# A routed attention and FFN kernel: one more head pair in cluster order, with smaller conversion buffers

## The chip, the core and the metric

The kernel runs on one core of a Trainium2 chip. A core has five engines with a queue each: PE (matmul; its weight loads are listed apart as PEld), DVE (vector), ACT (scalar), POOL (GpSimd) and SP, which here only issues DMAs. Each queue is worked off in its own order, and engines meet at semaphores. The metric is the device time of one execution in microseconds, the median of three runs.

## The reference

Two blocks follow each other. Attention with routing (4 batches, 8 heads, 768 tokens, 64 values per head): each query and key is assigned to the nearest of 16 centroids of its head, and a query sees only keys of its own cluster.

```python
q_assign = np.argmax(np.einsum('bhsd,hcd->bhsc', q_n, c_n), axis=-1)
k_assign = np.argmax(np.einsum('bhsd,hcd->bhsc', k_n, c_n), axis=-1)
mask = q_assign[:, :, :, None] == k_assign[:, :, None, :]
scores = np.where(mask, scale * np.matmul(q, k.transpose(0, 1, 3, 2)), -1e9)
attn = softmax(scores)                      # over the keys
out = np.matmul(attn, v)
```

Then an FFN on the 3072 rows of 512 values: `h = x @ w_in` (512 by 2048), `g = max(h, 0) + alpha * min(h, 0)`, `g @ w_out` (2048 by 512). The weights arrive as 64-bit floats, and the kernel makes 32-bit ones of them on the chip.

## The kernel before, in words

**Pairs and steps.** Two heads are worked on together: pairs 0 to 15, four to a batch. The program is a list of *steps* (`steps`), three to a pair and a half of its queries (384), and the loops over `u` at the end write out the order of everything by hand: each step has five slots, `load_at` and `prep_at` say which load and which preparation falls in which, and `later(k, piece)` puts a piece k slots ahead. Nothing is reordered afterwards: each engine's queue holds its instructions as the loops wrote them. Batch 0 is steps 0 to 23 (first loop: four pairs with their first halves, *block 0*, then the second halves, *block 1*), batch 1 steps 24 to 47, batch 2 steps 48 to 62, batch 3 steps 63 to 74.

**Two ways to do a pair.** In general a pair is done in halves: scores of 6 key chunks (128 keys) against 384 queries for both heads (`score`, L784), exponentials on ACT (L805), a mask on DVE (L825; in batch 0 two extra matmuls L793 put the mask into the scores), row sums on DVE (`add_up`, `turn`, `rows_sums`), products with v (`weigh`, L939), and `normalise` (L1042) into the tiles `xT` that the FFN reads. The accumulator `vps` has one buffer: PE can't start the next pair's products before `normalise` has read it. Pairs 9 to 15 (`n >= NO`) are done *in cluster order*: queries and keys are sorted by cluster, and each key chunk is only compared with a window of 224 to 384 queries (`window`, `weigh_near` L972). That takes three steps for both halves. It costs an ordering ahead of time: `order_features` (two transposes L567), `order_sims` (four matmuls L575), `order_counts` (argmax, a scan L589), `order_begins` (two matmuls L601), `order_ranks`, `order_rows`, `order_clusters` on DVE (L609 to L645), and then 24 indirect DMAs from POOL (`order_scatter`, L675), which write rows of q, k and v to a scratch in DRAM by rank. They take the rows from two stage tiles that SP loads (L661, three DMAs a tile). `pace()` (a one-element copy on ACT, L651, and one on POOL, L652) keeps POOL from running ahead. `order_load` brings the sorted rows back (L688, L697, L706). At the end six transposes on PE (L1002), twelve indirect DMAs (L1011) and four loads (L1023) put the result in the old order again. `order_constants` makes, once, what the ordering needs: on POOL two iotas (L508, L511) and three pairs of an iota (L521) and a product (L523), on DVE a reduction (L531), five small instructions (L538 to L548) and three `shifts`. `ORDERS` holds the step in which each ordering begins, `LEADS` how many steps ahead the sorted rows are loaded.

**The conversion of the weights.** 32 pieces of 128x512 (`convert`), numbered 0 to 31, in batch 0: SP loads a piece (L247, 512 KB) into one of five raw tiles; *split* (L253, L255, DVE) takes the exponent into a buffer `power` and the mantissa into the weight tile; *scale* (L259, L261, ACT); *join* (L265, L268, DVE), after which the raw tile is free; *multiply* (L271, POOL), after which `power` is free. Scale comes four slots after split, join two after scale. `fetch` issues a load when a raw tile is free in program order. The list `converting` gives the pieces begun in each step of block 0; from step 12 on two begin in each step. w_in and w_out alternate by fours.

**The FFN.** `feeds` says after which step the FFN of a half of a batch may begin, and its 28 pieces are spread over the steps of the next block: `hidden` (four matmuls L1066, a copy on ACT L1072, a slope on DVE L1058) and `final` (four matmuls L1084, evacuated at L1090 or L1092). The first FFN piece stands in step 12, right after the products of pair 3. Batch 3's FFN comes last, in another form with fewer products (L1246, L1302).

**Memory.** `first_part` holds what only batch 0 needs (members, raw tiles, `cvt` with the exponent buffers); when it closes after step 23, `second_part` takes its room for five more exponential tiles, one `xT` tile (`xmore`) and all that the ordering uses.

The line that decides whether a step finds its piece:

```python
later(4 if len(stages) == 2 else 2, lambda: stages and advance(stages))
```

## Time and profile before

| | |
|---|---|
| median of three runs | 932.17 us (932.1 to 932.6) |
| the profiled execution | 932.13 us, its span 930.4 us |
| PE busy | 916.0 us, 98% |
| DVE busy | 654.3 us, 70% |
| ACT busy | 262.2 us, 28% |
| POOL busy | 389.1 us, 42% |
| granted TensorE clock | 1.00 in all stretches |
| batch 0: block 0 ends, block 1 ends | about 77 us, about 201 us |

A row of a group, a line or the timeline gives the line of the kernel, the engine, the operation, what is written from what, and how often; "busy" is the time in which the engine worked, and in square brackets stands how long the engine was idle ahead of the row and who released it. Lines named L784 and so on are those of the kernel before.

### The profile page before, as it was taken

How to read it: one execution, taken by the hardware profiler on the slowest of the kernel's cores; microseconds unless marked ns; L12 is line 12 of the kernel's file. 1: busy time of each engine (PE TensorE's matmuls, PEld its weight loads, DVE VectorE, ACT ScalarE, POOL GpSimd, SP SyncE). 2: the span in 40 equal slices, each digit the busy share in tenths (PEclk: the TensorE clock that was granted, in tenths of full speed). 3: DMA queues.
4: the chain of work that ended last, by engine and by line, in shares of the span. 5: the costliest groups of instructions: out<-in, count | busy, mean ns of one | idle time of the engine just before them, and what ended most of it. 6: DMA issues, size and time to landing. Idle time of an engine off the chain costs nothing.

```text
span 930.4 us, 11983 instructions
## 1 busy us (share of the span) xinstructions
PE 916.0 (98%) x3963; PEld 494.6 (53%) x3963; DVE 654.3 (70%) x1246; ACT 262.2 (28%) x660; POOL 389.1 (42%) x579
## 2 busy tenths in 40 slices
PE   8999999999999999999999999999999999999997
PEld 5534444445445454455555554555555555556886
DVE  5797788889769699598997899764647135598200
ACT  5764454223123122232222332122222121221000
POOL 2433232200006768587766787677723470000000
PEclk9999999999999999999999999999999999999999
DMA  8433659028001625453762283643511012000000
GB/s 301 132 123 93 148 128 159 18 56 179 26 1 51 153 73 145 88 107 85 156 133 42 50 136 96 142 87 95 97 37 27 12 38 54 1 0 1 23 23 26
DMA packets 226708, 77.71 MB, mean 84 GB/s; under 512 B 210752, under 2 KB 214544, under 8 KB 226640
## 3 DMA queue, kind: packets, MB, share of 16 engines
q1 hardware_dynamic: 217728, 62.72, 30.6%
q0 software_dynamic: 8064, 13.78, 4.7%
q8 instruction: 33, 0.54, 0.3%
q10 hardware_dynamic: 848, 0.39, 0.2%
q14 instruction: 35, 0.29, 0.1%
HBM read 52.25 MB, written 24.25 MB: 82 GB/s over the span
## 4 chain that ended last, share of the span: by engine, by line
PE 94%; DVE 4%; issue 1%; POOL 0%; ACT 0%; DVEq 0%; ACTq 0%; POOLq 0%
PE fps L1066 27%; PE fps L1084 27%; PE sps L784 7%; PE vps L939 7%; PE sps L1302 4%; PE sps L1246 4%; PE fps L784 3%; PE vps L1246 2%; PE vps L1302 2%; PE vps L972 1%; PE mps L972 1%; PE fps L1302 1%; PE fps L1246 1%; PE sps L793 1%; PE mps L894 1%
## 5 line engine op out<-in xcount | busy, mean ns | idle before, releaser
L1066 PE MATMUL fps<-xT,w_in_sb 128*128 128x384 f32 x768 | 259.3, 491 | 0.0
L1084 PE MATMUL fps<-w_out_sb,gT 128*128 128x512 f32 x576 | 254.1, 595 | 0.3 <-DVE gT L1058 0.3
L675 POOL DMA_INDIRECT scratch<-stage,off x168 | 181.3, 1079 | 67.1 <-DMA stage<-in_v_dram 29.5
L1066 PEld LDWEIGHTS fps<-xT,w_in_sb 128*128 128x128 f32 x768 | 142.3, 190 | 103.2 <-issue 4.9
L1084 PEld LDWEIGHTS fps<-w_out_sb,gT 128*128 128x128 f32 x576 | 107.5, 190 | 132.2 <-issue 122.6
L1072 ACT COPY gT<-fps 128x384 f32<-128x384 f32 x96 | 46.0, 479 | 235.9 <-PE fps L1066 235.9
L652 POOL COPY paced<-pace 1x1 f32<-1x1 f32 x204 | 55.0, 270 | 135.7 <-ACT pace L651 135.2
L1058 DVE SCALAR_TENSOR_TENSOR gT<-gT,alpha 128x384 f32<-128x384 f32 x96 | 61.5, 648 | 60.8 <-ACT gT L1072 60.7
L1011 POOL DMA_INDIRECT back<-rows,off x84 | 85.6, 1018 | 22.2 <-issue 16.5
L784 PE MATMUL sps<-qkT 64*128 64x384 f32 (+1 forms) x464 | 85.0, 485 | 0.0
L805 ACT ACTIVATE E<-sps 128x768 f32<-128x768 f32 (+1 forms) x76 | 56.3, 786 | 62.1 <-PE sps L793 39.7
L784 PEld LDWEIGHTS sps<-qkT 64*128 64x128 f32 x464 | 41.2, 186 | 38.6 <-issue 15.5
L825 DVE SCALAR_TENSOR_TENSOR more<-aq,key,more 128x384 f32<-128x384 bf16 (+2 forms) x116 | 60.4, 579 | 0.0
L939 PE MATMUL vps<-E,vt 128*64 128x384 f32 x292 | 54.2, 495 | 1.5 <-DVE xT L1042 1.5
L271 POOL TENSOR_TENSOR w_in_sb<-w_in_sb,power 128x512 f32<-128x512 f32 x16 | 26.9, 1684 | 67.4 <-DVE w_in_sb L268 67.4
L271 POOL TENSOR_TENSOR w_out_sb<-w_out_sb,power 128x512 f32<-128x512 f32 x16 | 22.5, 1411 | 56.0 <-DVE w_out_sb L268 56.0
L825 DVE SCALAR_TENSOR_TENSOR E<-aq,key,E 128x384 f32<-128x384 bf16 (+2 forms) x88 | 45.0, 569 | 0.6 <-ACT E L802 0.6
L835 DVE TENSOR_TENSOR acc<-acc,E 128x768 f32<-128x768 f32 x35 | 33.3, 951 | 14.5 <-ACT E L805 13.6
L907 DVE RECIPROCAL inverses<-mps 64x12 f32<-64x12 f32 (+1 forms) x42 | 10.5, 249 | 45.7 <-PE mps L894 39.8
L1090 ACT COPY y<-fps 128x512 f32<-128x512 f32 x18 | 10.6, 587 | 99.2 <-PE fps L1084 99.2
L1092 DVE TENSOR_TENSOR y<-y,fps 128x512 f32<-128x512 f32 x24 | 16.4, 682 | 27.6 <-PE fps L1084 27.6
L805 ACT ACTIVATE more<-sps 128x768 f32<-128x768 f32 (+1 forms) x40 | 29.2, 764 | 12.2 <-PE sps L784 11.8
(284 smaller groups left out, 1174.1 us busy)
## 6 DMA issues: line engine op xcount, KB each, us to landing
raw<-in_moe_w_in_dram SPq DMA_DIRECT2D x16, 512.0 KB, 5.2
raw<-in_moe_w_out_dram SPq DMA_DIRECT2D x16, 512.0 KB, 4.3
out_dram<-y SPq DMA_DIRECT2D x21, 256.0 KB, 2.4
qk<-scratch SPq DMA_DIRECT2D x56, 96.0 KB, 3.5
qk<-in_q_dram SPq DMA_DIRECT2D x48, 96.0 KB, 3.6
qk<-in_k_dram SPq DMA_DIRECT2D x48, 96.0 KB, 3.6
w_in_kept<-w_in_sb SPq DMA_DIRECT2D x8, 512.0 KB, 3.3
vt<-in_v_dram SPq DMA_DIRECT2D x9, 384.0 KB, 6.5
```

What stands on the lines that cost most here:

```text
L652: nc.gpsimd.tensor_copy(out=sorts["paced"], in_=token)
L675: nc.gpsimd.indirect_dma_start(out=scratch[n][1][h * NX + xx], out_offset=bass.IndirectOffsetOnAxis(ap=ranks[n][:, xx, h:h + 1], axis=0), ...
L784: nc.tensor.matmul(out=bank(ps, h, m), lhsT=qkT[r:r + D, S + c * P:S + (c + 1) * P], rhs=qkT[r:r + D, tokens], start=True, stop=not early_ ...
L805: nc.scalar.activation(out=E[:, :, 0:m], in_=ps[:, :, 0:m], func=AF.Exp, scale=SCALE)
L825: nc.vector.scalar_tensor_tensor(out=e, in0=of, scalar=keys[n][:, NJ + c, h:h + 1], in1=e, op0=ALU.is_equal, op1=ALU.mult)
L939: nc.tensor.matmul(out=po[r:r + D, 0:HS], lhsT=vts[n][:, h, c, :], rhs=e[:, h, :], start=(c == 0), stop=(c == NJ - 1))
L1011: nc.gpsimd.indirect_dma_start(out=to[i], out_offset=bass.IndirectOffsetOnAxis(ap=place[:, h, j:j + 1], axis=0), in_=rows[j // HJ][:, j % ...
L1058: nc.vector.scalar_tensor_tensor(out=gs[f], in0=gs[f], scalar=alpha[:, f:f + 1], in1=gs[f], op0=ALU.mult, op1=ALU.max)
L1066: nc.tensor.matmul(out=ps[:, 0:HS], lhsT=w_in_sb[:, c, f * P:(f + 1) * P], rhs=xTs[b, half][:, c, :], start=(c == 0), stop=(c == NCH - 1))
L1084: nc.tensor.matmul(out=ps[:, 0:DM], lhsT=gs[f][:, i * P:(i + 1) * P], rhs=w_out_sb[:, f, :], start=on and f == f0, stop=off and f == f0 + ...
L1246: nc.tensor.matmul(out=bank[to], lhsT=w_in_form(m, x, cc), rhs=rhs[:, cc, :], start=start and cc == 0, stop=cc == KH - 1, skip_group_check ...
L1302: nc.tensor.matmul(out=bank[to], lhsT=g_form(m, x, t), rhs=w_out_form(n, x), start=start and x == 0, stop=x == NQ - 1, skip_group_check=no ...
```

## The change

- Pair 7, the last of batch 1, is done in cluster order too, ahead of pairs 4 to 6: `ORDERED` is 7 and 9 to 15. Batch 1 takes 21 steps and the program 72; the second half of batch 1 has 9 steps.
- Its ordering begins in step 11, `order_constants` is called in step 10 (before: step 25), and the first loop takes pieces from `sorting` too: in steps 16 to 20 five scatters a step. Tiles for the ordering are there from the start (`ordc`, `ordp`, `order`, `pace`), so the conversion gets three raw tiles in place of five, and `cvt` two exponent buffers in place of three. For the first 12 conversions every third takes its exponent buffer from the room of the output rows (`ypool`).
- Once more than 12 conversions have begun, scale comes three slots after split and join one after scale. `converting` in steps 3 to 6 is 1, 1, 1, 2 (before: 2, 0, 2, 1; the sum is the same).
- The later orderings begin in steps 26, 29, 32, 35, 38, 53 and 57. Which `xT` tile lies in which pool changes, a separate pool `ordx` holds the second half's factors, and some slots move by one.

```diff
-    NO = WHOLE * NCH - 3
+    ORDERED = [2 * NCH - 1] + list(range(WHOLE * NCH - 3, B * NCH))
+    NO = ORDERED[1]
...
-    cvt = first_part.enter_context(tc.tile_pool(name="cvt", bufs=3))
+    cvt = first_part.enter_context(tc.tile_pool(name="cvt", bufs=2))
...
-    raw_tiles = [raws.tile([P, CW, 2], U32, name=f"raw{i}") for i in range(5)]
+    started = [0]
+    raw_tiles = [raws.tile([P, CW, 2], U32, name=f"raw{i}") for i in range(3)]
...
-            power.append(cvt.tile([P, CW], U32, name="power"))
+            i = started[0]
+            started[0] += 1
+            power.append(ypool.tile([P, DM], FP32, name="y").bitcast(U32)
+                         if i < NCH * 3 and i % 3 == 2 else
+                         cvt.tile([P, CW], U32, name="power"))
...
-            later(4 if len(stages) == 2 else 2, lambda: stages and advance(stages))
+            later((4 if len(stages) == 2 else 2) - (started[0] > NCH * 3),
+                  lambda: stages and advance(stages))
...
-        whole = [n for n in range(b * NCH, (b + 1) * NCH) if n >= NO]
-        rest = [n for n in range(b * NCH, (b + 1) * NCH) if n < NO]
+        whole = [n for n in range(b * NCH, (b + 1) * NCH) if n in ORDERED]
+        rest = [n for n in range(b * NCH, (b + 1) * NCH) if n not in ORDERED]
...
-            pool = sorts["xmore"] if (b, half) == (WHOLE - 1, 1) else xpool
+            pool = sorts["xmore"] if (b, half) in ((1, 1), (B - 1, 0)) else xpool
...
-    ORDERS = [26, 29, 35, 38, 41, 56, 60]
-    LEADS = [4, 3, 4, 4, 3, 3, 3]
+    ORDERS = [11, 26, 29, 32, 35, 38, 53, 57]
+    LEADS = [3, 4, 3, 4, 4, 3, 3, 3]
...
+        if u == ORDERS[0] - 1:
+            order_constants()
...
-        converting = 0 if u < 0 else (2, 0, 2, 2, 0, 2, 1, 1, 1, 1, 1, 1)[u] if u < UB else 2
+        converting = 0 if u < 0 else (2, 0, 2, 1, 1, 1, 2, 1, 1, 1, 1, 1)[u] if u < UB else 2
...
+            if sorting:
+                pace()
+            room = 1 + (i < 2)
+            while sorting and room:
+                scatters, piece = sorting.popleft()
+                piece()
+                room -= scatters
...
-        if u == TOGETHER + 1:
-            order_constants()
```

More of the change, by code (lines that the diff above doesn't have):

```diff
@@ L76 @@
     fast.enter_context(tc.manual_schedule())
+    sorts = {name: fast.enter_context(tc.tile_pool(name=name, bufs=bufs)) for name, bufs in
+             (("ordc", 1), ("ordp", 1), ("order", B * NCH - 2 * NCH), ("pace", 8))}
     first_part = fast.enter_context(ExitStack())
@@ L490 @@
     STAGES = 2
-    us, ranks, orders, scratch, sorts = {}, {}, {}, {}, {}
+    us, ranks, orders, scratch = {}, {}, {}, {}
     sorting = deque()
@@ L496, in second_part @@
         first_part.close()
-        for name, bufs in (("emore", 1), ("ordc", 1), ("ordp", 1), ("order", NP - NO),
-                           ("xmore", 1), ("byrow", 1), ("pace", 8)):
-            sorts[name] = fast.enter_context(tc.tile_pool(name=name, bufs=bufs))
+        for name in ("emore", "ordx", "xmore", "byrow"):
+            sorts[name] = fast.enter_context(tc.tile_pool(name=name, bufs=1))
         for i in range(5):
@@ L560, in order_constants @@
             later(5 + i, piece)
-        begins = ordc.tile([P, NP - NO], FP32, name="begins")
+        begins = ordc.tile([P, len(ORDERED)], FP32, name="begins")
         sorts.update(stage=stage, number=number, place=place, before=before, within=within,
@@ L609, in order_ranks @@
         nc.vector.tensor_tensor(out=begin, in0=ps[:, 0:2], in1=sorts["shift"], op=ALU.add)
-        nc.vector.tensor_copy(out=sorts["begins"][:, n - NO:n - NO + 1], in_=ps[:, 0:1])
+        i = ORDERED.index(n)
+        nc.vector.tensor_copy(out=sorts["begins"][:, i:i + 1], in_=ps[:, 0:1])
         nc.vector.scalar_tensor_tensor(out=count, in0=count, scalar=begin[:, 1:2],
@@ L734 @@
         for half in range(2) if rest else ():
-            if half and not whole:
+            if half and b < WHOLE - 1:
                 begun_at.append(len(steps))
             steps += [(n, half, s) for n in rest for s in range(SB)]
-            feeds[len(steps)] = [(b, 0), (b, 1)] if whole else [(b, half)]
+            feeds[len(steps)] = [(b, half)] if b < WHOLE - 1 else [(b, 0), (b, 1)]
     begun_at.append(len(steps))
@@ L877, in rows_sums @@
     def rows_sums(n, half):
-        near = n >= NO
+        near = n in ORDERED
         if not near or half == 0:
@@ L911, in spread_out @@
     def spread_out(n, half, inv):
-        pool = sorts["ordp"] if n >= NO and half else rdp
+        pool = sorts["ordx"] if n in ORDERED and half else rdp
         rd = rds[n, half] = pool.tile([P, HS], FP32, name="rd")
@@ L1340, in room_for_y @@
         def room_for_y():
-            t = sorts["xmore"].tile([P, NCH, HS], FP32, name="xT").rearrange(
+            t = xpool.tile([P, NCH, HS], FP32, name="xT").rearrange(
                 "p c q -> p (c q)")
@@ L1374 @@
         if half is None:
-            t = ORDERS[n - NO]
+            t = ORDERS[ORDERED.index(n)]
             load_at.setdefault(t, []).append(lambda n=n: load(n))
@@ L1379 @@
             at(t + 2, 2, lambda n=n: order_sims(n))
-            load_at.setdefault(u - LEADS[n - NO], []).append(
+            load_at.setdefault(u - LEADS[ORDERED.index(n)], []).append(
                 lambda n=n: order_load(n))
-            at(u - 4, 0, lambda n=n: prep_clusters(n))
+            sooner = u - 1 < TOGETHER
+            at(u - 4, FIRST if u - 4 < TOGETHER else 0, lambda n=n: prep_clusters(n))
             for i in range(2):
-                at(u - 1, i, lambda n=n, i=i: order_blocks(n, i))
-                at(u - 1, FIRST + i, lambda n=n, i=i: order_queries(n, i))
+                at(u - 1, i + FIRST * sooner, lambda n=n, i=i: order_blocks(n, i))
+                at(u - 1, FIRST + i + sooner, lambda n=n, i=i: order_queries(n, i))
             continue
@@ L1393 @@
             else:
-                load_at.setdefault(u - (9 if u < 2 * TOGETHER else 10), []).append(
+                load_at.setdefault(u - (9 if u < start_of[NO, None] else 10), []).append(
                     lambda n=n: load(n))
@@ L1404 @@
             at(u - (3 if n < NCH else 5 if u - 6 < TOGETHER else 6), FIRST,
-               lambda n=n: prep_sims(n)) if u - 6 < 2 * TOGETHER else at(
+               lambda n=n: prep_sims(n)) if u < start_of[NO, None] else at(
                    u - 6, FIRST + 1, lambda n=n: prep_sims(n))
@@ L1424, in scatters_at @@
         if v < SB:
-            return 1 + (s == 0 or i == 0)
+            return 1 + (s == 0 or i % 3 == 0)
         if v < 3 * SB:
@@ L1429, in scatters_at @@
             return int(s == 0 or i == 0)
-        return 1 + (s == 0 or i % 2 == 0)
+        return 1 + (s == 0 or i != 1)
     def feed(pieces):
@@ L1611 @@
                             scalar2=good[:, 1:2], op0=ALU.is_le, op1=ALU.mult)
-    NN, m = NP - NO, 2 * NC
+    NN, m = len(ORDERED), 2 * NC
     spans = const.tile([m, 4, NN], FP32, name="spans")
```

## The prediction

> **What bounds the kernel now.** The busy line of the page comes first, then the same by stretch: 31 to 68 us (second half of block 0), 80 to 170 (block 1), 201 to 322 and 322 to 441 (batch 1, first and second half). Columns: stretch, its length, busy us of PE, PEld, DVE, ACT, POOL, the clock, DMA.
>
> ```profile
> PE 916.0 (98%) x3963; PEld 494.6 (53%) x3963; DVE 654.3 (70%) x1246; ACT 262.2 (28%) x660; POOL 389.1 (42%) x579
> ...
> 31.30:67.60 36.30, 33.43 (x316) 14.81 (x316) 33.79 (x72) 26.14 (x41) 12.71 (x8) 1.00 0.38 121
> ...
> 80.00:170.00 90.00, 89.75 (x352) 41.20 (x351) 72.94 (x123) 39.43 (x67) 23.20 (x16) 1.00 0.57 119
> 201.00:322.00 121.00, 121.00 (x442) 59.18 (x441) 95.90 (x178) 26.48 (x67) 36.65 (x59) 1.00 0.35 80
> 322.00:441.00 119.00, 117.57 (x465) 58.53 (x465) 101.07 (x182) 33.30 (x103) 82.57 (x120) 1.00 0.41 99
> ```
>
> From 80 us on PE never waits for long: the time is the sum of its matmuls. Before that DVE is as full (33.79 of 36.30), and PE waits for it. PE's timeline names the place and the next one that matters:
>
> ```profile
> 67.66 1.51 PE L939 MATMUL vps<-E,vt 128*64 128x384 f32 x8 [1.46 <-DVE xT L1042]
> ...
> 77.40 8.01 PE L1066 MATMUL fps<-xT,w_in_sb 128*128 128x384 f32 x24
> ```
>
> At 67.66 (step 10) PE had waited 1.46 us for the normalisation of pair 2. At 77.40 the first FFN piece begins; its fourth product reads what the normalisation of pair 3 writes, so that is due three products of 0.645 later, at 79.34. DVE's timeline between the two:
>
> ```profile
> 67.05 0.56 DVE L1042 TENSOR_TENSOR xT<-vps,rd 128x384 f32<-128x384 f32 x1
> 67.52 0.42 DVE L253 TENSOR_SCALAR power<-raw 128x512 uint32<-128x512 uint32 x1
> ...
> 70.67 0.70 DVE L268 SCALAR_TENSOR_TENSOR w_in_sb<-raw,w_in_sb 128x512 f32<-128x512 uint32 x1
> 72.54 1.49 DVE L253 TENSOR_SCALAR power<-raw 128x512 uint32<-128x512 uint32 x1 [1.17 <-POOL w_in_sb L271]
> ...
> 76.10 0.38 DVE L945 STREAM_TRANSPOSE simT<-fps 128x192 f32<-128x192 f32 x1 [0.53 <-PE fps L932]
> ...
> 78.40 0.56 DVE L1042 TENSOR_TENSOR xT<-vps,rd 128x384 f32<-128x384 f32 x1
> ```
>
> Pair 3 is ready at 78.96, only 0.4 us before PE needs it. What DVE gains in work or waits between these two L1042 beyond 0.4 us, PE loses.
>
> **What the Trainium skill says.** "Perfetto Trace Analysis", Tensor Engine Instruction: the end of a matmul in a profile is an estimate. So I price PE by distances between starts. "SBUF — State Buffer", Who interferes with whom: DVE and GpSimd share a pair of ports, an exclusive lock for whole instructions, for DVE instructions in a 2-port mode or with two SBUF inputs. The trace agrees: L253 took 1.49 us at 72.54 beside a POOL multiply and 0.42 otherwise, and two multiplies behind a run of DVE joins took 4.17 us (1.27 to 1.29 each alone). "TensorE: Matmul & The Clock Gate", Part 1: an idle window of about 3.4 us can halve the clock. No row here shows it (1.00 in all); a longer PE wait is created below, so up to 1.7 us more (an estimate by that page: half of one window) goes into the range. "DMA: Bandwidth & Descriptors", Issuing engines are not separate DMA queues: all queues end on the same 16 engines. A raw load lands in 3.5, 4.8, 8.4 us (least, median, most).
>
> **The change, part by part.**
>
> *Pair 7 ordered.* Between the starts of its PE work a half of an unordered pair takes 330.51 - 321.89 = 8.62 us, an ordered pair 498.17 - 491.01 = 7.16:
>
> ```profile
> 321.89 1.56 PE L784 MATMUL sps<-qkT 64*128 64x384 f32 x8
> ...
> 330.51 3.81 PE L1066 MATMUL fps<-xT,w_in_sb 128*128 128x384 f32 x11
> ```
>
> ```profile
> 491.01 1.29 PE L784 MATMUL sps<-qkT 64*128 64x224 f32 x8
> ...
> 498.17 2.41 PE L1084 MATMUL fps<-w_out_sb,gT 128*128 128x512 f32 x5
> ```
>
> Two halves become one: 17.24 - 7.16 = 10.08 saved. Added: six transposes L1002 (three in 0.33 us by starts: 0.66) and two products L601 (3.7/14 = 0.26 each). The four similarity products only change their line. Net **-8.9 us**, all on PE's path.
>
> *Its ordering moves into steps 11 to 20.* By its rows DVE gets 2 transposes L567 (0.96), argmax 3.1, the chain from L584 to L645 5.3: 10.3 us. In 80 to 170 DVE is idle 17 us, of which some 6 are waits for multiplies, so 11 are there for about 9.5 (durations overlap by 7%). It just fits; I put **+0.5** for bunching and take 0 to +6 as bounds. POOL gets 24 scatters (1.08), 13 pace copies, 6 stage copies: about 31 us in five steps that also hold ten multiplies (13 us), 44 of some 51. SP gets 18 stage loads between the raw loads, 8 loads of the order's input, and 12 loads of the ordered rows at step 21; the last wait for scatters, and what stands behind them (loads of pairs 4 and 5) is used two steps later, at some 10 us a step. ACT gets 13 copies of 0.19. Twelve row scatters L1011 (12 us of POOL) fall in steps 28 to 31, where POOL had little.
>
> *Batch 1's second half* now lasts nine steps with one pair less: DVE has more room there. The 1.43 us that PE waited at L575 (396.5 us) lies in it; I count half of that back, **-0.7**.
>
> *Raw tiles 5 to 3.* A split now waits for the load that could only start when the third last join ended. In the order of DVE's instructions the work between that join and the split was at least 6.7 us before; for conversions 6 and 10 it is now about 2.4 and 1.3, and for several others 4 to 5, against 3.5 to 5.2 for a load. Conversion 6 waits 2.5 or so, but takes the place of 3.3 us in which the old order collided with POOL (pairs of splits at 45.5 to 48.3). Conversion 10 stalls about 3.3 us in step 8, less two collisions of 1.07 that go; conversion 9 up to 0.7. This DVE time is ahead of the 67.05 normalisation, so PE waits for it: **+1.5** (1.0 if w_in loads land in 4.3, 2.5 at 5.2).
>
> *Constants of the order moved from step 25 to step 10.* Their POOL rows:
>
> ```profile
> 69.57 4.17 POOL L271 TENSOR_TENSOR w_in_sb<-w_in_sb,power 128x512 f32<-128x512 f32 x2 [3.46 <-DVE w_in_sb L268]
> ...
> 178.80 0.46 POOL L508 IOTA place<- 128x384 uint16 x1
> 179.21 0.13 POOL L511 IOTA number<- 128x12 int32 x1
> 204.80 0.28 POOL L521 IOTA simT<- 128x128 f32 x1 [25.45 <-DVE top L406]
> ...
> 206.83 0.46 POOL L523 TENSOR_TENSOR stage<-row,ident 128x128 f32<-128x128 f32 x1
> ```
>
> On POOL they stand behind the multiply of conversion 10, which gets the ports only when join 11 ends; DVE's next instruction, the reduction L531, waits for the last of them. From L1042 of pair 2: to the end of join 11 3.75 (67.52 to 71.27); that multiply 1.18 more (to 72.45); iotas and products 3.03 (178.80 to 179.34, 204.80 to 207.29); L531 0.57; five small instructions 1.3; join 12 1.2; shifts 0.25; split 13, its scaling on ACT and join 13, which now comes ahead of the normalisation, 2.5; L945 to L1042 2.86. Sum 16.6 against PE's 11.8: **+4.8** at the fourth product of the first FFN piece. Bounds 2.5 (the multiply gets in earlier) and 6.5 (ports, clock).
>
> *Edits at nothing.* The exponent buffer in the rows' room: its last multiply is over before the first row is written in step 13. Two exponent buffers after conversion 12, with scale and join one slot sooner: splits 17, 19, 21 stand about 1 us behind the join two before and wait 0.8 to 1.4 for the multiply; before, five splits waited 1.2 to 1.4. If scatters delay multiplies, this cover is gone (the slower rival). x tiles exchanged between two pools: each is read up before its next use, a block ahead.
>
> **Sum**: -8.9 - 0.7 + 1.5 + 4.8 + 0.5 = -2.8. The profiled execution took 932.13 (span 930.4, 1.7 around it), the median 932.17: 929.4.
>
> **The rivals.**
> 1. *The start's losses are hidden* (the loads land early, the multiply gets in between): only about 1 us of 6.8 is lost. 932.2 - 9.6 + 1 = 923.6. For it: the second L1042 has no other user than PE. Against: DVE's 33.79 of 36.30.
> 2. *Slower: POOL in steps 16 to 20.* Scatters wait for their stage loads, which SP issues after a raw load that waits for DVE; multiplies stand behind them, splits with two buffers behind these. It decides once a multiply is over 4 us late: then both splits of a step wait, about 2 us in each of five steps, and DVE's spare 1.5 us is used up. +7 on the forecast: 936. For it: 44 of 51 us without any waiting, and scatters waited 29.5 us in all for stages. Against: they are paced, five a step.
> 3. *No change*: the start costs its upper bounds (2.5 and 6.5): 932.1.
>
> **How the numbers follow.** Forecast 0.45 (927 to 931.5), rival 1 0.20, rival 2 0.25, rival 3 0.10. 0.2%, about what a measurement here can tell from no change, is 1.9 us. Faster: 0.35 of the forecast's 0.45, and 0.20: 0.55. Same: 0.10 and 0.07: 0.17. Slower: 0.28. The range 923.5 to 936.5 leaves out 0.08 of rival 1 below and 0.10 of rival 2 above; the forecast's own is 927 to 931.5.
>
> **What would show it.** PE's wait at L939 in step 10 grows from 1.46 to about 3; a new wait of about 5 us inside the first L1066, and DVE idle some 4 us ahead of L531, on POOL; about 9 us less PE work in all; DVE above 90% from 80 to 170 us with PE still full. Wrong if L531 doesn't wait or the first FFN piece starts without a gap (rival 1), or if PE waits for slopes and rows in steps 16 to 21 (rival 2).

## The result, and the profile after

The kernel after takes 948.7 us (median of four runs, 946.4 to 950.4) against 932.4 for the kernel before beside it (932.1 to 933.1): a ratio of 1.0171, 95% interval 1.0159 to 1.0184. The profiled execution took 946.44 us, its span 944.7, 14.3 more than the span before.

The busy line of the page of after, and then the engines by stretch (columns as in the prediction):

```profile
PE 913.9 (97%) x3931; PEld 494.7 (52%) x3931; DVE 657.3 (70%) x1245; ACT 259.4 (27%) x667; POOL 428.7 (45%) x634
```

```profile
78.60:95.40 16.80, 10.47 (x28) 5.50 (x26) 12.61 (x29) 3.59 (x6) 2.53 (x2) 0.80 0.49 92
84.80:91.40 6.60, 4.25 (x7) 2.47 (x8) 6.35 (x15) 0.48 (x1) 0.70 (x1) 0.51 0.27 87
146.00:164.60 18.60, 14.16 (x45) 6.27 (x44) 12.05 (x20) 4.63 (x9) 14.65 (x19) 0.91 0.69 150
153.00:156.50 3.50, 3.50 (x5) 1.36 (x5) 2.37 (x5) 1.88 (x4) 3.06 (x6) 0.52 0.49 191
```

PE has 32 matmuls fewer, but is busy only 2.1 us less, since some of them ran at half clock; and it is not full in two stretches in which it was full before. In each of these the clock falls to about half (0.51, 0.52) for a few microseconds, late in a wait or soon after it. The waits in PE's timeline of after:

```profile
68.87 1.51 PE L948 MATMUL vps<-E,vt 128*64 128x384 f32 x8 [1.70 <-DVE xT L1051]
...
78.61 2.20 PE L1075 MATMUL fps<-xT,w_in_sb 128*128 128x384 f32 x6
...
87.14 8.30 PE L1075 MATMUL fps<-xT,w_in_sb 128*128 128x384 f32 x18 [6.33 <-DVE xT L1051]
...
151.85 5.40 PE L1093 MATMUL fps<-w_out_sb,gT 128*128 128x512 f32 x8 [2.40 <-DVE y L1101]
...
161.87 2.85 PE L1075 MATMUL fps<-xT,w_in_sb 128*128 128x384 f32 x8 [2.04 <-DVE y L1101]
```

To book the loss by place I take from PE's timeline the start of `score` of each step; "stretch 12" runs from that of step 12 to that of step 13. Differences to before, in us; the last column is batch 1, from step 24 to the first score of batch 2 (243.8 before):

| kernel | start to 12 | 12 | 13 | 14-17 | 18 | 19-22 | 23 | sum to 24 | batch 1 |
|---|---|---|---|---|---|---|---|---|---|
| after | 0.7 | 8.8 | 1.7 | 0.3 | 6.5 | 1.0 | 0.6 | 19.6 | -7.0 |

With 0.5 us by which the first score itself came later and 1.2 us by which the last store came later, that makes the 14.3.

Most of the runs below are from chips on which the kernel before takes 948 to 959 us, so each ratio is to the kernel before on the same chip.

### The profile page after: what moved, and what is told of

Its sections match the earlier page's. It is cut to its first block, busy times and chain, and to the rows that moved or that the text cites. A ratio compares the mean times of both kernels' runs of the same rounds, so it can differ in the third digit from the quotient of the medians.

```text
span 944.7 us, 12071 instructions
## 1 busy us (share of the span) xinstructions
PE 913.9 (97%) x3931; PEld 494.7 (52%) x3931; DVE 657.3 (70%) x1245; ACT 259.4 (27%) x667; POOL 428.7 (45%) x634
## 4 chain that ended last, share of the span: by engine, by line
PE 81%; DVE 11%; issue 2%; DMA 2%; ACT 1%; POOL 1%; SPq 1%; ACTq 0%; DVEq 0%; POOLq 0%
PE fps L1075 23%; PE fps L1093 23%; PE sps L793 5%; PE sps L1311 4%; PE sps L1255 4%; PE vps L948 4%; PE fps L793 2%; PE vps L1255 2%; PE vps L1311 2%; DVE acc L844 2%; DMA raw<-in_moe_w_in_dram 1%; PE vps L981 1%; PE mps L981 1%; PE fps L1311 1%; PE fps L1255 1%
## 5 line engine op out<-in xcount | busy, mean ns | idle before, releaser
L1075 PE MATMUL fps<-xT,w_in_sb 128*128 128x384 f32 x768 | 261.4, 494 | 8.4 <-DVE xT L1051 6.3
L684 POOL DMA_INDIRECT scratch<-stage,off x192 | 204.2, 1064 | 79.5 <-issue 30.2
L1075 PEld LDWEIGHTS fps<-xT,w_in_sb 128*128 128x128 f32 x768 | 143.5, 191 | 113.2 <-issue 14.5
L661 POOL COPY paced<-pace 1x1 f32<-1x1 f32 x217 | 60.5, 279 | 149.1 <-ACT pace L660 143.9
L1020 POOL DMA_INDIRECT back<-rows,off x96 | 99.3, 1035 | 21.9 <-issue 18.4
L1067 DVE SCALAR_TENSOR_TENSOR gT<-gT,alpha 128x384 f32<-128x384 f32 x96 | 57.7, 611 | 65.2 <-ACT gT L1081 65.2
L793 PE MATMUL sps<-qkT 64*128 64x384 f32 (+1 forms) x448 | 82.1, 482 | 0.7 <-ACT E L814 0.6
L793 PEld LDWEIGHTS sps<-qkT 64*128 64x128 f32 x448 | 40.1, 186 | 37.0 <-issue 14.2
L834 DVE SCALAR_TENSOR_TENSOR more<-aq,key,more 128x384 f32<-128x384 bf16 (+2 forms) x110 | 56.0, 569 | 0.6 <-ACT more L811 0.6
L834 DVE SCALAR_TENSOR_TENSOR E<-aq,key,E 128x384 f32<-128x384 bf16 (+2 forms) x82 | 41.9, 565 | 0.0
L279 POOL TENSOR_TENSOR w_in_sb<-w_in_sb,power 128x512 f32<-128x512 f32 x13 | 18.3, 1404 | 51.2 <-DVE w_in_sb L276 51.2
L1101 DVE TENSOR_TENSOR y<-y,fps 128x512 f32<-128x512 f32 x24 | 16.4, 682 | 28.4 <-PE fps L1093 28.4
L660 ACT COPY pace<-ones 1x1 f32<-1x1 f32 x217 | 31.2, 184 | 11.1 <-POOL paced L661 10.5
```

The costliest lines, as they stand in the source:

```text
L661: nc.gpsimd.tensor_copy(out=sorts["paced"], in_=token)
L684: nc.gpsimd.indirect_dma_start(out=scratch[n][1][h * NX + xx], out_offset=bass.IndirectOffsetOnAxis(ap=ranks[n][:, xx, h:h + 1], axis=0), ...
L793: nc.tensor.matmul(out=bank(ps, h, m), lhsT=qkT[r:r + D, S + c * P:S + (c + 1) * P], rhs=qkT[r:r + D, tokens], start=True, stop=not early_ ...
L834: nc.vector.scalar_tensor_tensor(out=e, in0=of, scalar=keys[n][:, NJ + c, h:h + 1], in1=e, op0=ALU.is_equal, op1=ALU.mult)
L1020: nc.gpsimd.indirect_dma_start(out=to[i], out_offset=bass.IndirectOffsetOnAxis(ap=place[:, h, j:j + 1], axis=0), in_=rows[j // HJ][:, j % ...
L1067: nc.vector.scalar_tensor_tensor(out=gs[f], in0=gs[f], scalar=alpha[:, f:f + 1], in1=gs[f], op0=ALU.mult, op1=ALU.max)
```

## The experiments

On the slower chips the traces show extra waits and a lower clock, nearly all of it from 440 us on. So the evidence is the stretches before step 24, in which unchanged parts take the same time on every chip, nearly all within 0.1 us. The column for batch 1 is less sure: e1_buffers, which leaves batch 1 as it was, shows +0.8 there, a wait of 0.78 us for which the profile names no reason. The stretches are those of one profiled execution of each kernel, the ratio is that of all its runs. Differences to before, as above; in the first column from the first score on:

| kernel | start to 12 | 12 | 13 | 14-17 | 18 | 19-22 | 23 | sum to 24 | batch 1 | ratio to before (95%) |
|---|---|---|---|---|---|---|---|---|---|---|
| e1_buffers | 1.0 | 1.7 | 1.2 | 0.0 | 0.0 | 0.0 | 0.0 | 3.9 | +0.8 | 1.0040 (1.0022-1.0058) |
| e10_raw3 | 0.2 | 0.0 | 0.0 | 11.2 | 0.2 | 6.3 | 0.0 | 18.0 | 0.0 | 1.0183 (1.0149-1.0217) |
| e2_const12 | 0.8 | 1.6 | 2.0 | 0.3 | 9.3 | -0.8 | 0.6 | 13.8 | -7.0 | 1.0107 (1.0069-1.0144) |
| e11_constm2 | 7.3 | 1.1 | 1.7 | 0.5 | 1.0 | 0.4 | 0.6 | 12.5 | -7.4 | 1.0071 (1.0043-1.0099) |
| e3_nostage | 0.6 | 9.5 | 1.7 | 0.5 | 1.5 | -0.4 | 0.6 | 14.0 | -6.0 | 1.0081 (1.0051-1.0112) |
| e4_load4 | 0.8 | 9.4 | 1.7 | 0.3 | 8.4 | -0.8 | 0.6 | 20.5 | -8.3 | 1.0167 (1.0138-1.0195) |
| e5_rawact | 2.4 | 0.1 | 2.0 | 0.5 | 1.5 | 1.8 | 0.6 | 8.8 | -8.3 | 1.0056 (1.0035-1.0077) |
| e6_early | 0.8 | 1.4 | 2.0 | 0.4 | 7.0 | -0.7 | 0.6 | 11.5 | -7.0 | 1.0087 (1.0061-1.0113) |
| e7_both | 2.4 | 0.1 | 2.0 | 0.4 | 1.5 | 1.7 | 0.6 | 8.7 | -8.3 | 1.0059 (1.0036-1.0081) |
| e8_long | 1.2 | 0.1 | 4.5 | 0.5 | 1.5 | 3.5 | 0.6 | 11.8 | -7.6 | 1.0061 (1.0038-1.0084) |
| e9_scat320 | 2.4 | 0.0 | 2.0 | 0.4 | 1.0 | 1.0 | 0.6 | 7.4 | -7.7 | 1.0016 (0.9994-1.0039) |
| e13_even | 1.2 | 1.0 | 0.3 | 0.3 | 0.2 | 1.9 | 6.8 | 11.8 | -7.3 | 1.0051 (1.0038-1.0065) |
| e14_evenlong | 1.3 | 0.1 | 0.3 | 0.3 | 0.3 | 0.4 | 6.3 | 8.9 | -8.3 | 1.0029 (1.0020-1.0037) |
| e15_even21 | 1.2 | 0.1 | 0.3 | 0.3 | 0.2 | 2.4 | 1.9 | 6.5 | -8.3 | 0.9994 (0.9986-1.0002) |
| e16_even20 | 1.3 | 0.1 | 0.3 | 0.4 | 2.5 | 3.2 | 0.6 | 8.5 | -8.3 | 0.9982 (0.9971-0.9992) |
| e17_back | 0.8 | 0.0 | 0.3 | 0.5 | 2.5 | 0.9 | 0.6 | 5.6 | -5.4 | 0.9983 (0.9964-1.0002) |

**The smaller buffers alone** in the kernel before (the hunks of the change for `cvt`, `raw_tiles`, `power.append`, `later` and `converting`, and no other):

> The kernel before with the conversion's smaller buffers alone: three raw tiles, two exponent buffers and the room of the output rows for every third of the first 12, scale and join one slot sooner after conversion 12, the new list of conversions begun; pair 7 stays unordered and the constants stay in step 25. Theory A (the ordering's stage loads and scatters make block 1 late, the buffers alone cost only what they cost at the start): the second normalisation comes some 1.2 us later, as in the kernel after (68.82 against 67.61), block 1 loses at most 1 us more: 933 to 934.5 us. Rival B (two exponent buffers and three raw tiles are too few for block 1 by themselves): some 8 us more between steps 14 and 24, PE waits for rows and slopes there: 940 to 942 us.

Block 1 loses nothing (0.0 in stretches 14 to 23): theory A. But the start costs 3.9 us, not 1.5: PE waits 1.46 us in step 12 for the normalisation of pair 3, ahead of which join 13 now stands, and 1.47 us in step 13 for a slope.

**Raw tiles alone** in the kernel before:

```diff
-    raw_tiles = [raws.tile([P, CW, 2], U32, name=f"raw{i}") for i in range(5)]
+    raw_tiles = [raws.tile([P, CW, 2], U32, name=f"raw{i}") for i in range(3)]
```

> The kernel before with three raw tiles in place of five, and nothing else: three exponent buffers, the old distances between split, scale and join, the old list of conversions begun. The smaller buffers together cost 3.9 us up to step 24: 1.0 to 1.2 up to the score of step 12, 1.7 in step 12 (join 13 ahead of the normalisation) and 1.2 in step 13. Theory A (the raw tiles cost what lies up to step 12, the shorter distances and two exponent buffers the rest): 1 to 2 us up to step 12, under 0.5 us in steps 12 and 13: 933.5 to 934.5 us where before takes 932.4, a ratio of 1.001 to 1.002. Rival B (the raw tiles cost it all): 3.5 to 4.5 us, of them 2 to 3 in steps 12 and 13, a ratio of 1.004 or more.

Neither theory: at the start three raw tiles cost 0.2 us, and in block 1 17.7. With the old distances a tile is held too long, and DVE waits ten times for a load between 100 and 200 us, 0.36 to 6.42 us each, as in this line of its timeline:

```profile
124.35 0.43 DVE L253 TENSOR_SCALAR power<-raw 128x512 uint32<-128x512 uint32 x1 [6.42 <-DMA raw<-in_moe_w_out_dram]
```

e1_buffers has three tiles too and loses nothing there. What it does otherwise is the shorter distances, one exponent buffer fewer and another order of conversions 3 to 6; only the first lets a tile go sooner. So the shorter distances, with which 2.9 us are lost in steps 12 and 13, are what makes three tiles enough. No run changes the distances alone.

**The constants in step 12**, behind the normalisation of pair 3:

```diff
-        if u == ORDERS[0] - 1:
+        if u == UB:
             order_constants()
...
-        brief = asg.tile([P, HS], FP32, name="simT")
+        brief = ypool.tile([P, DM], FP32, name="y")[:, 0:HS]
```

> The kernel after with the constants of the order made in step 12, behind the normalisation of pair 3, in place of step 10 (their short-lived rows lie in an output-row tile for that). Theory A: PE's wait of 6.33 us inside the first FFN piece goes, and with it the stretch of low clock (0.71 from 87 to 95 us) and the 1.15 us at 105: between the scores of steps 12 and 14 the kernel after lost 8.8 and 1.7 us, so about 10 us come back, less 1 to 2 us for the constants' DVE work in block 1: 938 to 941 us. Rival B (the wait is made by splits and joins that lie ahead of the normalisation in any case, the constants only fill DVE's idle time): at least 3 us of the wait stay, 944 us or more.

Stretch 12 falls from 8.8 to 1.6, what the buffers cost without any constants: theory A for that place, 7.2 us for the constants in step 10. The total is worse than expected, since stretch 18 went from 6.5 to 9.3: PE's two waits there are 1.1 us longer (3.50 and 2.07), and each of them is followed by half clock, where after has it only behind the first. How the 6.33 us came about, in DVE's timeline of after:

```profile
70.94 1.49 DVE L263 TENSOR_SCALAR w_out_sb<-raw 128x512 uint32<-128x512 uint32 x1
...
75.51 0.55 DVE L539 TENSOR_REDUCE cols<-stage 128x3 f32<-128x384 f32 x1 [1.87 <-POOL stage L531]
76.09 1.61 DVE L546 TENSOR_SCALAR simT<-row,cols 128x128 f32<-128x128 f32 x1
...
80.62 1.40 DVE L261 TENSOR_SCALAR power<-raw 128x512 uint32<-128x512 uint32 x1
...
86.44 0.56 DVE L1051 TENSOR_TENSOR xT<-vps,rd 128x384 f32<-128x384 f32 x1
```

The wait for POOL's rows is 1.87 us, not 4.2: the multiply ahead of them began at 70.77, right behind its own join and not after the next, and DVE still had a split and that next join to do until 73.64. But three DVE instructions stood beside a POOL instruction and took 1.40 to 1.61 us for 0.3 to 0.4.

The constants ahead of step 0 (to be compared with e9_scat320 below, which has them in step 12; their short-lived rows lie where after has them):

```diff
-        if u == UB:
+        if u == -2:
             order_constants()
```

> The last kernel with the constants two steps ahead of step 0, where POOL and DVE have little to do, in place of step 12. Theory A (their five DVE instructions in steps 12 and 13 delay a slope there: step 13 took 2.0 us more than before with them, 1.2 without): step 13 loses at most 1.3 us, the start at most 0.5 us more: 0.5 to 1 us better than with the constants in step 12. Rival B (the start has no room either, the first scores come later by what the constants take): the first score of step 1 comes 2 us or more later, no gain.

Stretches 0 and 1 lose 3.95 and 1.61 us: rival B.

**Stage loads left out**, so that pair 7's scatters carry zeros:

```diff
-        for src, p0, d0 in ((q, 0, 0), (k, TS, 0), (v, TS, D)):
+        for src, p0, d0 in () if n < NO else ((q, 0, 0), (k, TS, 0), (v, TS, D)):
```

> The kernel after without the 18 loads that bring pair 7's rows into the stage tiles: its scatters write zeros, so the attention of pair 7 is computed from zeros; all else is issued as before. Scatters no longer wait for loads, and no raw load stands behind a stage load that waits for a scatter. Theory A (stage loads are the link: SP's queue holds the raw loads up, scatters wait for stages with multiplies behind them): most of the 8.4 us lost between the scores of steps 14 and 24 come back: 941 to 944 us. Rival B (the scatters' own 24 times 1.06 us on POOL delay the multiplies enough): under 2.5 us come back, 946 us or more.

Stretches 14 to 23 lose 2.2 us in place of 8.4: theory A. The scatters are all still there, so their time on POOL is not the main thing. What the stage loads do can be read on SP, whose queue in after says (columns: start, duration, queue, line, operation, count):

```profile
138.92 0.61 SPq L670 DMA_DIRECT2D stage<-in_v_dram  x1
147.45 0.60 SPq L670 DMA_DIRECT2D stage<-in_q_dram  x1
...
149.45 1.07 SPq L251 DMA_DIRECT2D raw<-in_moe_w_in_dram  x2
...
158.12 2.25 SPq L130 DMA_DIRECT2D qk<-in_q_dram  x4
160.47 2.22 SPq L130 DMA_DIRECT2D qk<-in_k_dram  x4
162.79 0.57 SPq L251 DMA_DIRECT2D raw<-in_moe_w_in_dram  x1
```

The third stage load waits from 139.5 to 147.45 for the first four scatters. Behind it stand two raw loads whose tiles had been free since the joins ended at 141.6 and 146.8; then come eight loads of q and k, at 0.56 us each, ahead of the next raw load. DVE answers, in its timeline of after:

```profile
149.39 1.47 DVE L261 TENSOR_SCALAR power<-raw 128x512 uint32<-128x512 uint32 x1 [2.64 <-POOL w_out_sb L279]
...
154.13 0.43 DVE L261 TENSOR_SCALAR power<-raw 128x512 uint32<-128x512 uint32 x1 [2.34 <-DMA raw<-in_moe_w_in_dram]
...
167.58 0.44 DVE L261 TENSOR_SCALAR power<-raw 128x512 uint32<-128x512 uint32 x1 [4.40 <-DMA raw<-in_moe_w_in_dram]
```

and the evacuations of rows (L1101) behind these splits are what PE waits for at 151.85 and 161.87.

**Pair 4's loads of q and k in step 15**, ahead of the stage loads:

```diff
-                load_at.setdefault(u - (9 if u < start_of[NO, None] else 10), []).append(
+                load_at.setdefault(u - (12 if n == NCH else 9 if u < start_of[NO, None] else 10), []).append(
```

> The kernel after with the eight loads of pair 4's q and k issued in step 15, ahead of the ordering's stage loads, in place of step 18. In the trace of the kernel after they stood on SP from 158.1 to 162.7 us, ahead of two raw loads, and DVE then waited 4.40 us for a raw tile at 167.58. Theory A: that wait falls under 1 us, PE's waits of steps 18 and 21 shrink, 2 to 4 us come back: 944.5 to 947 us. Rival B (the raw loads are late because of the stage loads alone): the wait stays, no change, 948 to 950 us.

The wait of 4.40 us is gone, as theory A said, and the later stretches improve (19 to 22 from +1.0 to -0.8). But DVE now waits 3.28 us for a scaling of ACT, and stretch 18 gets worse by 1.9: PE's second wait there is 2.29 us and is followed by half clock, in after it was 2.04 us and was not. Nothing is gained in all, which fits rival B's number, not its reason.

**The raw loads off SP's queue**, on top of the constants in step 12:

```diff
-        nc.sync.dma_start(out=raw.rearrange("p n w -> p (n w)"), in_=src)
+        queue = nc.scalar if begun[0] + len(fetched) >= NCH * 3 + 2 else nc.sync
+        queue.dma_start(out=raw.rearrange("p n w -> p (n w)"), in_=src)
```

> The kernel with the constants in step 12, and the raw loads from conversion 14 on issued from ACT's queue in place of SP's, so that none stands behind a stage load or a load of q and k. In the kernel with the constants in step 12 alone, the stretch from the score of step 18 to that of step 19 took 21.45 us (before: 12.15), DVE waited there 3.73 us for a multiply and 2.56 and 4.12 us for raw tiles. Theory A (two links, multiplies behind scatters and raw loads behind SP's other loads): the two waits for raw tiles go, the one for the multiply stays with PE's first wait of 3.50, the stretch takes 16 to 18 us. Rival B (the raw loads are late only since what frees the tiles is late): the waits for raw tiles stay, 20 us or more. Against before on the same chip: about 4 us better than with SP's queue, a ratio of 1.004 to 1.007 where the kernel with the constants in step 12 had 1.0107.

Stretch 18 takes 13.66 us: it loses 1.5 in place of 9.3. Theory A, and more than expected: the waits for raw tiles are gone, and of the one for a multiply 0.99 us is left. The second comes from the other direction: the first stage loads no longer stand behind a raw load that waits for its tile, and the first scatter is held up for 0.29 us, in e2_const12 for 4.27. All loads still run, so it is their order in the queue that counts, not what they move. (On ACT's queue the loads cost something too: the 1.6 us of stretch 12 only move to stretch 11, where PE waits 1.54 us for an exponential.) PE's timeline at the same two instructions:

```profile
143.81 3.70 PE L1094 MATMUL fps<-w_out_sb,gT 128*128 128x512 f32 x8 [0.48 <-DVE y L1102]
...
150.78 2.85 PE L1076 MATMUL fps<-xT,w_in_sb 128*128 128x384 f32 x8 [0.69 <-DVE y L1102]
```

**The first stages early**, on top of the constants in step 12, and together with the other queue:

```diff
-            if i < 2 * PARTS:
+            if i < 2 * PARTS and (n >= NO or i >= STAGES):
...
+    for i in range(STAGES):
+        load_at.setdefault(ORDERS[0] + 3, []).append(lambda i=i: order_stage(ORDERED[0], i))
```

> The kernel with the constants in step 12, and the first two stage tiles of pair 7 loaded in step 14 (they need no ranks), not with the first scatters in step 17. In the kernel with the constants in step 12 the first scatter waited 4.27 us for them, and the multiplies of step 17 stood behind it. Theory A: the first scatter no longer waits, the multiply is on time (DVE's wait of 3.73 falls under 1.5), SP's third stage load goes out some 4 us sooner and the raw loads with it; the stretch from the score of step 18 to that of step 19 takes 13 to 16 us; what remains is the raw load behind the eight q and k loads. Rival B (five scatters a step are too much for the multiplies in any case): over 18 us.

> The two changes together: raw loads on ACT's queue from conversion 14 on, and the first two stage tiles loaded in step 14, the constants in step 12. Theory A (constants, late first stages and raw loads behind SP's other loads are together the whole loss of the kernel after beyond the smaller buffers' 3.9 us at the start): the stretch from the score of step 18 to that of step 19 takes 12.2 to 13.5 us, that from step 14 to step 24 at most 1.5 us more than before; then the pair in cluster order gives 7 us in batch 1 and the kernel ends 2 to 3 us ahead of before, a ratio of 0.996 to 0.999. Rival B (scatters take POOL from the multiplies even so): 3 us or more stay in block 1, a ratio of 1.000 or above.

Alone it takes 2.3 us out of stretch 18. The first scatter is held up for 0.29 us and no wait for a multiply is left there, but DVE waits 5.15 us for a raw tile at 158.82, and 7.0 us stay: rival B's number, not its reason. On top of the other queue it takes out nothing, since the first stage loads are early there in any case; 4.3 us stay in stretches 14 to 23, and that is rival B. So e5_rawact undid both directions, and e6_early tells them apart: stage loads late behind a raw load were 2.3 of the 9.3 us, raw loads late behind stage loads and loads of q and k the larger part.

**Scatters in the first two slots** on top of e5_rawact:

```diff
-            room = 1 + (i < 2)
+            room = (3, 2, 0)[i]
```

> The kernel with the constants in step 12 and the raw loads on ACT's queue, and the five scatters of a step in the first two slots (three and two, in place of two, two and one), so that POOL has a slot free ahead of the next step's multiplies. There, DVE still waited 3.61 us for a multiply at 163.55 and 1.31 us at 176.41, and step 21 took 2.05 us more than before. Theory A (what is left in block 1 is multiplies behind the last scatters of the step before): steps 18 to 22 lose at most 1.5 us against before in place of 3.3; about 2 us better, a ratio of 1.001 to 1.004 where it had 1.0056. Rival B (POOL's total load is what counts, not where the scatters stand): no change, 3 us or more stay.

Stretches 18 to 22 lose 2.0 in place of 3.3: 1.3 us better where theory A said about 2. The kernel is level with before (its interval holds 1).

**Long distances for conversions 12 and 13** on top of e7_both:

```diff
-            later((4 if len(stages) == 2 else 2) - (started[0] > NCH * 3),
+            later((4 if len(stages) == 2 else 2) - (started[0] > NCH * 3 + 2),
```

> The last kernel, and conversions 12 and 13 keep the long distances between split, scale and join (four and two slots), so that join 13 stands behind the normalisation of pair 3 and not ahead of it. With the smaller buffers alone PE waited 1.46 us there for the normalisation (the stretch from the score of step 12 to that of step 13 took 13.78 us, before 12.09) and 1.47 us for a slope one step later. Theory A: both waits shrink, 12.1 to 12.6 us for that stretch, 1.5 to 2.5 us off the time of the kernel without it, a ratio of 0.994 to 0.997 against before. Rival B (the split itself, which waits for a multiply, is what is late): the stretch stays over 13.4 us.

Neither theory: in e7_both stretch 12 had no loss left to save (0.1), its loss was in stretch 11. There it saves 1.1 us, but step 13 is worse by 2.5, since PE waits 2.26 us for a slope behind joins and splits and half clock follows, and stretches 19 to 22 by 1.7, again with half clock, behind a wait of 1.98 us.

**The late conversions spread** on top of e9_scat320; then with the long distances too; then ended earlier (only the list's second half differs):

```diff
-        converting = 0 if u < 0 else (2, 0, 2, 1, 1, 1, 2, 1, 1, 1, 1, 1)[u] if u < UB else 2
+        converting = 0 if u < 0 else (2, 0, 2, 1, 1, 1, 2, 1, 1, 1, 1, 1,
+                                            1, 1, 2, 2, 2, 2, 1, 2, 2, 2, 1, 0)[u]
```

> The kernel with the constants in step 12, the raw loads on ACT's queue and the scatters in the first two slots, and the last 18 conversions begun as 1, 1, 2, 2, 2, 2, 1, 2, 2, 2, 1 in steps 12 to 22 in place of two in each of steps 12 to 20. Theory A (the load of two conversions a step beside the ordering makes what is left): step 13 loses under 0.7 us against before in place of 2.0, steps 18 to 22 under 1 us in place of 2.0; up to step 24 the loss falls from 7.4 to 4.5 to 5.5 us, less than the 7.0 to 8.3 us that batch 1 gives back: a ratio of 0.996 to 0.999 against before. Rival B (the slopes are late for their place in the order, not for DVE's load): 7 us or more stay, 1.001 or above.

> The last kernel, with conversions 12 and 13 at the long distances of four and two slots, so that join 13 comes behind the normalisation of pair 3. With two conversions a step that took the loss of 1.6 us out of steps 11 and 12 but put 2.5 us more into step 13, where a slope came late behind joins and splits. Theory A (with one conversion in each of steps 12 and 13 the slope is in time): steps 11 and 12 lose under 0.6 us, step 13 under 1 us: 1 to 1.5 us better than the kernel without it, 0.995 to 0.998. Rival B (the joins move in front of the slope in any case): step 13 loses 2 us or more, no gain.

> The last kernel with its 18 late conversions begun as one in each of steps 12 and 13 and two in each of steps 14 to 21, so that the last begin one step sooner, and six of the last nine sooner. Theory A (the wait of 3.89 us in step 23 comes from weights that are converted too late for the last hidden pieces): step 23 loses under 1 us against before in place of 6.3, up to step 24 the loss is 3 to 4.5 us, and batch 1 gives back 8.3: 928 to 930 us where before takes 932.4 to 933, a ratio of 0.995 to 0.998. Rival B (the load only moves to the end of the block): step 23 keeps 4 us or more, 1.002 or above.

> The same with one conversion in step 12, two in each of steps 13 to 20 and one in step 21: half a step sooner than the kernel beside it, one conversion fewer than the kernel with two in every step where the slope of step 13 was late. Theory A: step 13 loses 0.3 to 1.5 us, step 23 0.6, up to step 24 3 to 5 us in all, a ratio of 0.995 to 0.999. Rival B: step 13 loses 2.5 us or more as with two conversions in step 12, 1.000 or above.

Steps 12, 13 and 18 lose 0.1, 0.3 and 0.3 us in e14_evenlong. For steps 13 and 18 it was the load of two conversions a step, since e13_even has the same there; step 12 needs the long distances too. But weights begun as late as step 22 bring a wait of 3.89 us for a slope in step 23. With the last begun in step 21 that stretch loses 1.9, with one more of them moved ahead 0.6; in return stretches 18 to 22 lose 2.6 and 5.7 us, where e14_evenlong lost 0.7. e15_even21 is level with before (932.0 against 932.7 us), e16_even20 ahead of it by 0.18% (931.5): the only version whose interval lies below 1, by less than the 0.2% that the prediction set as its bound. The two are not told apart by these runs. Of theory A's sums none came: up to step 24 it was 11.8, 6.5 and 8.5 us in e13_even, e15_even21 and e16_even20, for 4.5 to 5.5, 3 to 4.5 and 3 to 5. That the ratio of e16_even20 lies in its range is in part luck, then; 1.7 of its 8.5 us are half clock in the execution that was profiled, which took 1.8 us more than the median. e14_evenlong is 2.9 us better than e13_even up to step 24, where theory A said 1 to 1.5, and misses the ratio all the same. A wait is new in e15_even21 and e16_even20, 2.11 us of PE in step 20; ACT's queue in e16_even20 shows it:

```profile
166.59 5.46 ACTq L252 DMA_DIRECT2D raw<-in_moe_w_out_dram  x2
172.10 0.19 ACT L661 COPY pace<-ones 1x1 f32<-1x1 f32 x1 [5.79 <-DMA stage<-in_k_dram]
172.20 0.22 ACT L458 CAST every<-mps 128x96 bf16<-128x96 f32 x1
```

Two raw loads hold ACT's queue for 5.46 us, and a copy that PE needs (L458) stands behind them. **The last five raw loads back on SP's queue:**

```diff
-        queue = nc.scalar if begun[0] + len(fetched) >= NCH * 3 + 2 else nc.sync
+        queue = nc.scalar if 14 <= begun[0] + len(fetched) < 27 else nc.sync
```

> The last kernel (one conversion in step 12, two in each of steps 13 to 20, one in step 21) with only the raw loads 14 to 26 on ACT's queue and the last five on SP's again. Theory A (a load that waits on ACT's queue holds the copy for PE behind it): PE's wait of 2.11 us for the copy goes, step 20 loses under 0.5 us in place of 2.4: 1 to 3 us better, a ratio of 0.995 to 0.998. Rival B (the loads only move the wait to DVE, since they stand behind stage loads again): no gain, step 20 or 21 keeps 2 us or more.

PE's wait for the copy is gone, and the stretches to step 24 are 2.9 us shorter. But step 20 still loses 1.7 us, behind a wait for a slope, so theory A holds for the wait alone, and the ratio is the same with a wider interval, which holds 1. Batch 1 gives back 2.9 us less: PE waits 1.56 us at L1076, where four other kernels have waits of 0.56 to 0.94 us without a named reason, and 1.3 us go to a wait for an exponential that the last bullet of the next section tells of.

**The wait alone**: the kernel before with DVE held up ahead of the normalisation of pair 3.

```diff
+        if u == UB:
+            for _ in range(5):
+                nc.vector.tensor_reduce(out=idle, in_=w_in_sb[:, 0, 0:CW], axis=AX.X, op=ALU.max)
         if ended:
             normalise(*prior[:2])
```

> The kernel before with five reductions of 128x512 added on DVE (some 0.6 to 0.7 us each, 3 to 3.5 us) right ahead of the normalisation of pair 3 in step 12, into a tile that nobody reads. PE then waits some 2.6 to 3.1 us for the normalisation inside the first FFN piece, as it waited 6.33 us in the kernel after. Theory A (a wait of that length is followed by about 3 us of halved TensorE clock, as after the waits of 2.40 and 6.33 us there): step 12 takes 4 to 5 us more than before, 1.4 to 1.7 us of them in products that run at half speed once the wait is over. Rival B (the clock fell for another reason, the wait alone counts): step 12 takes 2.6 to 3.1 us more, the clock stays at 1.00.

```profile
82.90 6.04 PE L1067 MATMUL fps<-xT,w_in_sb 128*128 128x384 f32 x18 [2.76 <-DVE xT L1043]
```

PE waited 2.76 us, stretch 12 took 3.0 us more, and the clock stayed at 1.00: rival B for this wait. Its length alone doesn't decide; the last section shows what the clock went by.

## Why the prediction was wrong

It said 929.4 us, and that 936.5 was high enough; it took 948.7. Its places were mostly right: PE's waits in steps 10, 12 and 16 to 21 are where it looked. The profiled execution took 17.0 us more than forecast: 7.9 from block 1, 4.0 from step 12, 1.7 from step 13, 2.6 from batch 1, 1.7 at the two ends, less 0.8 up to step 12. The sum failed in four terms.

- **"+0.5 for bunching", block 1.** Measured 8.4 us in stretches 14 to 23, more than the bound of 6. Rival 2 had the place, the direction and nearly the price (7 more, 0.25 of the chance). Its mechanism, stage loads behind a raw load and then multiplies behind scatters, was the smaller part (2.3 of 9.3 us in e6_early). The larger link runs the other way: raw loads behind a stage load that waits for scatters. The prediction counted SP's new loads and said what stands behind the loads of step 21, but not what stands behind each stage load: the raw loads, which three tiles leave no time for. With the raw loads on another queue the loss in stretch 18 went from 9.3 to 1.5; the prediction had noted only that all queues end on the same engines. That POOL had 44 of 51 us to do can have mattered for 3.3 us at most, what stretches 18 to 22 lose in e5_rawact; moving the scatters took 1.3 of them.
- **"+4.8", constants.** Stretch 12 lost 8.8, of which 7.2 are the constants (without them in step 10 it loses 1.6). The term also holds join 13 ahead of the normalisation, so the 8.8 stand against it. Between the two normalisations DVE took 18.2 us (68.82 to 87.00) in place of 16.6, and PE's wait was 6.33, within the bound of 6.5; but its parts were others, less waiting for POOL and more beside POOL's instructions. What is beyond is the clock: 6.8 us at half speed, 4.6 us of them while PE worked, so some 2.3 us lost, where the prediction had kept 1.7 in the range and nothing in the sum.
- **"Edits at nothing", scale and join one slot sooner.** In e1_buffers 2.9 us are lost in steps 12 and 13. The 1.7 of step 12, where join 13 moved ahead of the normalisation, the prediction had in its +4.8; the 1.2 of step 13 (1.7 in after), where joins moved ahead of a slope, it had nowhere. **"+1.5", raw tiles**, was too much at the start (0.7 up to step 12 in after, 0.2 for raw tiles alone; the wait in step 10 grew to 1.70, not to about 3), and it never asked what three tiles cost in block 1: the shorter distances that it priced at nothing save most or all of 17.7 us there.
- **"-8.9" and "-0.7".** Batch 1 got 7.0 us shorter in after and 8.3 in several of the others. The pair in cluster order brings waits of its own that the row from 491 to 498 us, between two such pairs, doesn't have; PE's timeline of after:

```profile
218.03 0.80 PE L793 MATMUL fps<-qkT 64*128 64x320 f32 x2 [0.71 <-ACT more L811]
...
221.53 0.53 PE L793 MATMUL fps<-qkT 64*128 64x320 f32 x1 [0.53 <-ACT more L811]
...
252.76 0.85 PE L392 MATMUL mps<-qkT,cT 128*32 128x384 f32 x8 [0.57 <-DVE qk L987]
...
262.50 1.06 PE L583 MATMUL mps<-qk,cT 128*32 128x384 f32 x8 [0.62 <-ACT rows L1014]
```

That is 2.4 us of waits, and by starts the second of them costs more than its row says: from L793 to L392 PE takes 3.1 us with it (220.20 to 223.28) and 1.8 without it in e5_rawact (209.90 to 211.67), so 1.3 and not 0.53. The wait of 1.43 us at L575 is gone whole, not by half. Then -8.9 - 1.4 + 3.2 is -7.1 where 7.0 was measured, and without that one wait -8.4, where e5_rawact and five others that lack it show 8.3.

Two signs that it named were seen: the gap inside the first L1066 (after: L1075) and PE waiting for slopes and rows in block 1, which it had called the mark of rival 2. DVE was not above 90% from 80 to 170 us but at 81% (72.8 of 90 us): it stood waiting. PE's wait in step 10 grew to 1.70 and not to about 3, and DVE was idle 1.87 us ahead of the reduction and not some 4. What remains open: the last three kernels lose 5.6 to 8.5 us up to step 24 and give back 5.4 to 8.3; how much of that loss better slots could still save was not tried.

## What to carry to other kernels

When a transfer is added to a queue and must wait for another engine, list what stands behind it in that queue and how long each of those can be late: it is the buffers there that decide, not the time of the transfer. A buffer that is made smaller has to be priced for every stretch in which it is used, together with the distances that set how long it is held. And take a stretch's own waits into the price of work that is moved there, not only its matmuls.

## What was not expected of the hardware

The half clock comes in whole windows of 3.413 us. In every trace with several stretches at half clock they start whole multiples of that apart (after: at 84.88, 153.15 and 941.63 us, 20 and 231 windows), and ahead of the last one, at the end of the program, each lasts one, two or three windows; one costs 1.7 us where PE has work. Where the windows lie in the program differs from trace to trace (the first begins 2.96 us into the span in after, 0.11 in e3_nostage).

In these traces it goes by how long PE is idle within one window, counted from the stretches at half clock of the same trace. In the first 260 us of the traces PE is idle for 1.98 us or more in 20 windows, and after all 20 the next is at half clock. Of 35 windows at full clock with 1.2 to 1.9 us idle it follows one (1.73 us, in e9_scat320), of those with less none. Waits of 1.98 to 2.76 us, taken by their length, are followed by it in only 7 of 12, since some of the others lie across two windows. The engines in such windows, of e12_delay, e8_long and e5_rawact in turn (columns as in the prediction, the clock is third from the end):

```profile
78.11:81.52 3.41, 2.03 (x6) 0.89 (x6) 3.27 (x6) 0.40 (x1) 0.00 (x0) 1.00 0.20 83
81.52:84.93 3.41, 2.03 (x7) 1.26 (x8) 3.38 (x8) 0.48 (x1) 0.00 (x0) 1.00 0.00 0
```

```profile
176.53:179.94 3.41, 1.43 (x7) 0.44 (x4) 2.94 (x4) 1.43 (x3) 3.13 (x5) 1.00 0.00 0
179.94:183.35 3.41, 3.41 (x5) 1.35 (x4) 3.36 (x10) 2.33 (x4) 2.64 (x5) 0.50 0.13 42
```

```profile
174.75:178.16 3.41, 2.15 (x14) 0.60 (x12) 2.10 (x4) 0.24 (x1) 3.39 (x5) 1.00 0.15 43
178.16:181.58 3.42, 2.71 (x7) 1.27 (x8) 3.39 (x9) 3.42 (x6) 2.68 (x5) 1.00 0.11 36
```

The wait of 2.76 us in e12_delay leaves PE idle 1.38 us in each of two windows, and the clock stays at 1.00. A wait of 1.98 us lies in one window in e8_long, and the next is at half clock; in e5_rawact a wait of the same length lies across two, and the clock stays. The border is not exact, as the ends of matmuls are estimates: after 260 us, half clock follows 9 of 26 windows with 1.2 to 1.9 us idle.

The Trainium skill, "TensorE: Matmul & The Clock Gate", Part 1, says that the gate watches a free-running activity window of about 3.4 us; the traces agree in its length and in that its phase is not the program's. That a gap has to be as long as the window does not hold here: 2 us can be enough.
